# Taking 37 filler products out of the start of an attention and MoE kernel, and putting four ahead of it

## The chip, the cores and the metric

The kernel runs on one core of one Trainium2 chip. The metric is device time in microseconds (us), from one launch; smaller is better. Before the change the median of three runs is 240.69 us (239.54 to 241.6).

## The reference

What is computed is a Nyström approximation of attention over 8 batches of 8 heads (576 positions, head size 64, 32 landmarks), followed by a two-layer network with SiLU between its layers (512 to 2048 to 512). Cut to what matters:

```python
q_lm = q.reshape(B, H, m, S // m, D).mean(axis=3)      # m = 32 landmarks
k_lm = k.reshape(B, H, m, S // m, D).mean(axis=3)
A  = softmax(scale * q    @ k_lm.T)                    # 576 x 32 per head
Bm = softmax(scale * q_lm @ k_lm.T)                    # 32 x 32
C  = softmax(scale * q_lm @ k.T)                       # 32 x 576
Z  = Bm.T / (norm1(Bm) * norminf(Bm) + 1e-6)
for _ in range(6):
    Z = 2 * Z - Z @ Bm @ Z
x = A @ Z @ C @ v                                      # heads side by side: 4608 x 512
h = x @ w_in
out = (h * sigmoid(h)) @ w_out
```

All inputs and the output are float32; the kernel works in bfloat16 and float16 inside.

## The kernel before

The eight batches run one behind the other in a software pipeline. Of each batch, all 8 heads are kept as two groups of four heads by 32 landmarks, that is 128 partitions. In the first two batches TensorE forms the landmark sums itself; in later ones VectorE does, by adding halves.

**The order of the work is written out by hand.** The string `SEQUENCE` (lines 19 to 157) lists every step of every engine. `Plan.run` (line 204) walks through it, gives each step that needs PSUM the first free bank of seven (later eight), and hands the list to the program. Each engine executes its own steps in the order of the string and waits at each for its inputs; nothing is reordered. TensorE's weight load can run ahead of its products, its products can't run ahead of each other.

The names around the change, each with its batch behind the dot:

- `ldk` loads a block of keys (1) or queries (0) of batch 0 by SyncE's queue, in float32, into space that later holds `gm`; `kc` casts it, a part on ScalarE and a part on VectorE. `ld`, `ldv`, `wi` and `wo` load later batches, values and weights by GpSimd's queue.
- `lms` are the landmark sums: products of the identity with 64 columns of a position, summed in PSUM, six to a step. `tr` are transposes on TensorE (line 527), `trc` their copies to SBUF.
- `lmc` copies the sums, `ltr` transposes them by a product with the identity, `lmT` copies that. From `lmT` come the scores: `sb` (landmarks by landmarks), `A` (queries by landmarks) and `C` (landmarks by keys).
- `pb`, `Ax` and `Cx` are the exponentials on ScalarE (lines 647, 753, 798); `S` sums over a head on TensorE; `Ln` and `Rs` (lines 763, 767) turn the sums into reciprocals on ScalarE; `etn` is the normalized A.
- `ns`, `nsd` and `fb` are the six steps of the iteration for Z: a small product on TensorE, then two operations on VectorE, each waiting for the one before.
- `ctm` and `ctc` transpose and copy C's exponentials, `cv` is C by v, `wc` scales it, `zbd` and `zt` multiply it by Z, `m` multiplies that by `w_in`, and `mc` copies the result.
- `h` and `hx` are the first layer (A by `m`), `g` and `gx` its SiLU on ScalarE (lines 923 and 946). Behind them stands the second layer.

**Fillers.** A word such as `*5` in the string stands for five fillers, one behind the other (line 214). A filler is one product of a zero matrix (128 by 128) with 256 columns of zeros, written to PSUM bank 7, which no other step uses until the second layer begins. Nothing reads its result:

```python
    P.filler = Op("warm", [("PE", 0.11)],
                  lambda e: mm(banks[7][:, 0:256].rearrange("p (a x) -> p a x", a=2), zer,
                               bc(zer, 2, 1)))
```

Its operand `zer` is set once, by VectorE, at the start (line 445). A filler therefore waits for no other engine beyond that, and none waits for it; it only takes a place in TensorE's order. There are 64: 15 ahead of the first landmark sum `lms100.0`, six ahead of the sums of the second key block, six ahead of those of the first query block, and 37 behind `lms0112.0`, the last landmark sum of batch 0. In the profile a filler is a product on line 337 that writes `ps` and reads `zer`.

Of the kernel before, what the change touches and what calls it, by code (L numbers as in the profile page):

```python
# [28 lines left out]
ctc00.0/DVE tr05.1 trc05.1/ACT tr00.1 trc00.1/ACT Rs1.0 Rs0.0 ns11.0 nsd11.0 fb10.0 fb21.0 tr19.1
trc19.1/DVE ltr0.1 lms100.1 lms106.1 ns10.0 nsd10.0 lms1012.1 tr014.1 lms110.1 lms116.1  # L30
trc014.1/DVE ns21.0 tr114.1 lmT0.1/ACT wi1a wi0a wi1b1 wi1b0 wi3b0 wi3a lms1112.1 lmc1.1/ACT
tr10.1 trc10.1/ACT tr15.1 *2 ltr1.1 lmT1.1/ACT fb20.0 nsd21.0 etn1.0 trc15.1/DVE ns20.0 fb31.0 *3
ns31.0 ctm10.0 trc114.1/ACT etn0.0 nsd31.0 sb.1 pb.1 *1 A.1 Ax01.1 Ax00.1 nsd20.0 fb30.0 pbs.1
wrc.0 *1 ns30.0 nsd30.0 ctc10.0/DVE fb40.0 pbr.1 fb41.0 bmx.1 bmt.1 wi3b1 Ax11.1 Ax10.1 *5 C.1
Cx00.1 Cx11.1 Cx01.1 *1 ns40.0 nsd40.0 ns41.0 nsd41.0 fb50.0 fb51.0 cv0.0 cv1.0 wc.0 S01.1 Ln01.1
ns50.0 nsd50.0 *2 ns51.0 bbd.1 nsd51.0 zbd.0 S11.1 Ln11.1 S00.1 Ln00.1 wi2b0 wi2b1 wi2a ldv0.1
ldv1.1 *5 zt.0 ztc.0/DVE S10.1 ctm00.1 ctc00.1/DVE Rs0.1 Ln10.1 Cx10.1 *2 m1.0 mc11.0/ACT
mc10.0/DVE m0.0 f0.1 mc01.0/DVE mc00.0/ACT *1 ctm10.1 ctc10.1/DVE Rs1.1 csb.1 *1 h4.0 n1.1 m3.0
nrm.1 stz.1 stf0.1 mc31.0/DVE fb00.1 g4.0 mc30.0/DVE h2.0 g2.0 h6.0 g6.0 h0.0 g0.0 h3.0 ns00.1
wrc.1 nsd00.1 fb10.1 h5.0 g5.0 m2.0 mc21.0/ACT mc20.0/DVE *1 h13.0 g13.0 ns10.1 nsd10.1 fb20.1  # L40
h15.0 hx0.0 g15.0 ns20.1 nsd20.1 fb30.1 h9.0 g9.0 h11.0 g11.0 etn0.1 ns30.1 nsd30.1 fb40.1 hx8.0
gx8.0 g3.0 h8.0 h12.0 g12.0 etn1.1 ns40.1 nsd40.1 fb50.1 gx0.0 h10.0 g10.0 ld1.2 tr15.2
trc15.2/DVE h14.0 g14.0 ns50.1 nsd50.1 zbd.1 ldv2.1 cv0.1 wc.1 tr114.2 trc114.2/DVE tr19.2
trc19.2/DVE zt.1 g8.0 ztc.1/ACT tr10.2 trc10.2/DVE lra1.2 h7.0 g7.0 m3.1 mc31.1/ACT mc30.1/ACT
m1.1 mc11.1/DVE mc10.1/ACT h1.0 g1.0 ld0.2 tr00.2 lrb1.2 tr09.2 tr014.2 trc014.2/DVE tr05.2
trc05.2/DVE trc09.2/DVE lrc1.2 trc00.2/ACT h12.1 g12.1 h7.1 g7.1 h15.1 m2.1 mc20.1/ACT m0.1
mc00.1/ACT mc21.1/ACT mc01.1/ACT wo0 o0@5001.0 h14.1 g14.1 g15.1 o0@5000.0 fold lrd1.2 lra0.2
lrb0.2 lrc0.2 lrd0.2 h11.1 g11.1 ltr0.2 ltr1.2 lmT1.2/DVE lmT0.2/ACT ss00@5020.0 ss10@5020.0
ss20@5020.0 ss30@5020.0 wo1 h5.1 o1@5000.0 sb.2 pb.2 pbs.2 pbr.2 bmx.2 bmt.2 wo2 wt00 bbd.2 h8.1
h3.1 o1@5001.0 o2@5000.0 wo3 o2@5001.0 wt01 g8.1 csb.2 o3@5001.0 oc@5001.0/ACT g3.1 g5.1 n1.2  # L50
nrm.2 stz.2 o3@5000.0 hx8.1 f0.2 gx8.1 h0.1 g0.1 oc@5000.0/ACT h2.1 h10.1 g10.1 h4.1 h1.1 g2.1
g1.1 wt11 wt21 stf0.2 fb00.2 ns00.2 h13.1 g13.1 wt31 nsd00.2 fb10.2 wt10 wt20 wt30 p1@5020.0
c1@5020.0/ACT ns10.2 nsd10.2 fb20.2 h9.1 h6.1 g4.1 g9.1 g6.1 ss00@5100.0 p5@5020.0 c5@5020.0/DVE
hx0.1 gx0.1 ss10@5100.0 l1done.0 C.2 Cx00.2 Cx10.2 p6@5020.0 u2@5020.0/DVE ld100.3 ld101.3 ld110.3
ld111.3 ldv1.3 xt10.3<ldv1.3 xt11.3<ldv1.3 ns20.2 nsd20.2 ss20@5100.0 p3@5020.0 c12@5020.0
p7@5020.0 ld000.3 ld001.3 ld010.3 ld011.3 xt01.3<ldv1.3 xt00.3<ldv1.3 ldv0.2 ldv2.2 ldv1.2
l1done.1 A.2 Ax01.2 Cx11.2 ct1.2<ldv1.3 Ax10.2 Ax11.2 p1@5100.0 c1@5100.0/ACT Ax00.2 Cx01.2
ct0.2<ldv1.3 os@5000.0 ld100.4<ct0.2 ld101.4 ld110.4 ld111.4 lra1.3 fb30.2 ns30.2 p2@5020.0
# [1114 lines left out]
```

## Time and profile before

| | |
|---|---|
| runs | 240.69 us median, 239.54 to 241.6 |
| profiled execution, its own time | 239.41 us |
| its span, first to last instruction | 237.4 us |
| mean granted TensorE clock in the span | 0.996 |
| TensorE busy, fillers included | 231.4 us (97%) |
| ScalarE busy | 182.1 us (77%) |
| VectorE busy | 183.0 us (77%) |
| fillers, products | 64, median 273 ns each, from 1.1 to 31.0 us |

[...] "PE" is TensorE, "PEld" its weight loads, "DVE" VectorE, "ACT" ScalarE, "POOL" GpSimd, "SP" SyncE. Times in the views count from the start of the span. In the timeline a row merges equal instructions: start, length, engine, line, operation, what it writes and reads, and the count; in brackets how long the engine had been idle before it, and what ended that.

### The profile page before, as it was taken

The page shows a single profiled execution, that of the slowest core. Times are in us where ns is not written, and L with a number is a line of the kernel's source. Part 1 is how long each engine was busy: PE and PEld are TensorE (multiplying, and loading weights), DVE is VectorE, ACT ScalarE, POOL GpSimd, SP SyncE. Part 2 cuts the span into 40 slices and gives each one's busy share as a digit, 9 for nine tenths or more (in the row PEclk, how much of TensorE's full clock was granted, in tenths as well). Part 3 has the DMA queues.
Part 4 walks back from the last instruction along what each step waited for, and adds up shares of the span by engine and source line. Part 5 has one row for each costly group of instructions (what it writes and reads, how often), then busy time and mean ns, then how long its engine had stood idle before and what let it go on. Part 6 is the DMA issues. An engine that isn't in the chain of part 4 may idle for free.

```text
span 237.4 us, 7504 instructions
## 1 busy us (share of the span) xinstructions
PE 231.4 (97%) x2948; PEld 164.5 (69%) x2948; DVE 183.0 (77%) x508; ACT 182.1 (77%) x433; POOL 49.6 (21%) x89
## 2 busy tenths in 40 slices
PE   7999999999999999999999999999999999999993
PEld 5987556456877645687878655768876746789882
DVE  2689989898998669949999789858998665447752
ACT  3599999989889988996857998999779897812200
POOL 0936641240055004403060084000000000000000
PEclk9999999999999999999999999999999999999998
DMA  6999999999989996999999999995427450012355
GB/s 251 267 203 186 204 210 207 207 206 179 166 149 205 222 230 128 189 191 174 200 154 214 178 157 231 202 171 121 91 68 100 115 122 0 4 44 48 76 136 144
DMA packets 56163, 37.72 MB, mean 159 GB/s; under 512 B 37056, under 2 KB 47552, under 8 KB 56128
## 3 DMA queue, kind: packets, MB, share of 16 engines
q0 software_dynamic: 15168, 17.18, 44.4%
q1 hardware_dynamic: 40288, 19.28, 39.3%
q10 hardware_dynamic: 672, 0.79, 1.1%
q8 instruction: 23, 0.38, 0.7%
q14 instruction: 12, 0.10, 0.1%
HBM read 36.70 MB, written 9.44 MB: 194 GB/s over the span
## 4 chain that ended last, share of the span: by engine, by line
PE 84%; DMA 6%; ACT 4%; DVE 2%; SPq 2%; issue 1%; DVEq 0%; ACTq 0%
PE ps L337 81%; DMA out_dram<-ost 5%; PE ps L527 3%; SPq L988 2%; DMA gm<-in_k_dram 1%; DVE etn L772 1%; ACT L1126 1%; ACT ln L767 1%; ACT m L347 0%; ACT pb L652 0%; ACT ln L763 0%; ACT qk L347 0%; ACT et L753 0%; PE ps L813 0%; ACT gx L946 0%
## 5 line engine op out<-in xcount | busy, mean ns | idle before, releaser
L923 ACT ACTIVATE gm<-ps 128x512 f16<-128x512 f32 x128 | 68.1, 626 | 4.6 <-PE ps L337 4.4
L337 PE MATMUL ps<-etn,m 128*128 128x64 bf16 (+1 forms) x512 | 71.2, 286 | 0.1
L337 PEld LDWEIGHTS <-gm 128*128 128x128 f16 x512 | 48.8, 98 | 11.0 <-issue 1.0
L337 PE MATMUL ps<-w_out_sb,gm 128*128 128x256 f16 (+1 forms) x392 | 52.5, 281 | 0.0
L337 PEld LDWEIGHTS <-m 128*128 128x128 bf16 x512 | 31.4, 98 | 23.1 <-issue 2.8
L337 PEld LDWEIGHTS <-ss 128*128 128x128 f16 x408 | 38.4, 98 | 7.8 <-issue 1.8
L337 PE MATMUL ps<-wt,ss 128*128 128x256 f16 x272 | 34.9, 273 | 0.0
L1046 DVE TENSOR_TENSOR ost<-ost,ps 128x256 f32<-128x256 f32 x51 | 20.7, 416 | 10.5 <-PE ps L337 7.2
L347 ACT COPY ost<-ps 128x256 f32<-128x256 f32 (+1 forms) x45 | 17.3, 391 | 12.0 <-PE ps L337 11.8
L349 DVE CAST m<-ps 128x512 bf16<-128x512 f32 x29 | 18.8, 685 | 3.6 <-PE ps L337 3.5
L347 ACT CAST m<-ps 128x512 bf16<-128x512 f32 x35 | 18.9, 607 | 2.1 <-PE ps L337 2.1
L418 POOL DMA_DIRECT2D v<-in_v_dram x24 | 14.7, 621 | 27.9 <-PE ps L337 17.1
L721 DVE SCALAR_TENSOR_TENSOR st<-st,ps 128x128 bf16<-128x128 bf16 (+2 forms) x54 | 13.7, 257 | 7.8 <-PE ps L337 6.8
L401 POOL DMA_DIRECT2D qk<-in_k_dram x20 | 10.6, 545 | 36.6 <-DMA qT<-qk 16.5
L337 PE MATMUL ps<-w_out_sb,ss 128*128 128x256 f16 x136 | 17.6, 273 | 0.0
L349 DVE COPY ost<-ps 128x256 f32<-128x256 f32 x25 | 10.5, 421 | 7.1 <-PE ps L337 6.6
L946 ACT ACTIVATE gx<-ps 128x512 f16<-128x512 f32 x16 | 9.9, 622 | 7.5 <-PE ps L337 7.3
L337 PE MATMUL ps<-wt,gm 128*128 128x256 f16 x120 | 15.5, 272 | 0.0
L696 DVE TENSOR_TENSOR fb<-st,hmask 128x256 bf16<-128x256 bf16 (+1 forms) x54 | 14.5, 274 | 1.1
L401 POOL DMA_DIRECT2D qk<-in_q_dram x20 | 10.6, 548 | 20.3 <-issue 12.2
L798 ACT ACTIVATE ce<-ps 128x288 bf16<-128x288 f32 x32 | 12.9, 420 | 2.3 <-PE ps L337 2.3
L763 ACT ACTIVATE ln<-ps 128x288 f32<-128x288 f32 x32 | 12.3, 428 | 3.0 <-PE ps L337 2.8
(93 smaller groups left out, 347.6 us busy)
## 6 DMA issues: line engine op xcount, KB each, us to landing
out_dram<-ost SPq DMA_DIRECT2D x130, 64.0 KB, 2.0
v<-in_v_dram POOLq DMA_DIRECT2D x24, 192.0 KB, 7.7
qk<-in_k_dram POOLq DMA_DIRECT2D x20, 144.0 KB, 6.3
qk<-in_q_dram POOLq DMA_DIRECT2D x20, 144.0 KB, 6.1
w_out_sb<-in_moe_w_out_dram POOLq DMA_DIRECT2D x4, 512.0 KB, 15.1
gm<-in_k_dram SPq DMA_DIRECT2D x2, 576.0 KB, 3.9
gm<-in_q_dram SPq DMA_DIRECT2D x2, 576.0 KB, 6.8
qk<-in_q_dram POOLq DMA_DIRECT2D x2, 576.0 KB, 8.5
```

Source lines behind the costliest of these rows:

```text
L337: nc.tensor.matmul(out=out_ap, lhsT=lhsT, rhs=rhs, start=start, stop=stop, skip_group_check=True)
L347: nc.scalar.copy(out=out, in_=in_)
L349: nc.vector.tensor_copy(out=out, in_=in_)
L401: lambda e, t=t, g=g, h=h, src=src: nc.gpsimd.dma_start(out=qk_r[b % 2][64 * h:64 * h + 64, t, g].rearrange("p j d -> p (j d)"), in_=src[b ...
L418: lambda e, a=a: nc.gpsimd.dma_start(out=v_r[b % 2][a * L:(a + 1) * L, :, :], in_=v[b].rearrange("h (l a x) d -> a l h (x d)", l=L, a=VA)[ ...
L696: nc.vector.tensor_tensor(out=fb[it % 2][:, g0:g1], in0=bc(sr[it % 3][:, g0:g1, 0:L], 4, 2), in1=bc(hmask, n, 1), op=OP.mult), [o], 14.5 + ...
L721: nc.vector.scalar_tensor_tensor(out=s2[:, g0:g1, lo:SW], in0=s[:, g0:g1, lo:SW], scalar=2.0, in1=ps[:, 0:NG * SW].rearrange("p (g x) -> p ...
L763: lambda e, g=g, c=c, ln=ln: nc.scalar.activation(out=ln[:, c], in_=bank(me["S", g, c])[:, 0:HS], func=AF.Ln),
L798: nc.scalar.activation(out=ce[:, :, 0:VP].rearrange("p (i c) (a l) -> p c a i l", c=2, a=VA)[:, c], in_=bank(me["C"], 2 * g + c)[:, 0:HS]. ...
L923: lambda e, dc=dc, cell=cell: nc.scalar.activation(out=gm[:, dc, :], in_=bank(cell["o"]), func=AF.Silu),
L946: lambda e, d0=d0, cell=cell, c=c: nc.scalar.activation(out=gx[:, d0:d0 + 8, c:c + 64], in_=bank(cell["o"]).rearrange("p (c x) -> p c x", ...
L1046: nc.vector.tensor_tensor(out=out_, in0=x, in1=y, op=OP.add)
```

## The change

Only the string changes. All words with a star behind `lms0112.0` go: one filler ahead of `ltr0.0`, six ahead of `sb.0`, five ahead of `C.0`, two ahead of `ltr1.1`, three ahead of `ns31.0`, one each ahead of `A.1` and `ns30.0`, five ahead of `C.1`, one ahead of `ns40.0`, two ahead of `ns51.0`, five ahead of `zt.0`, two ahead of `m1.0`, one each ahead of `ctm10.1`, `h4.0` and `h13.0`. The first `*15` becomes `*19`. The two `*6` between them stay. So 31 fillers are left of 64. All other words keep their order, and so their PSUM banks; the rest of the diff is the text running over to other lines.

```diff
-ldk10 ldk11 ldk00 ldk01 const ident kc10ACT kc10DVE kj10 *15 lms100.0 tr15.0 tr10.0 trc10.0/DVE
+ldk10 ldk11 ldk00 ldk01 const ident kc10ACT kc10DVE kj10 *19 lms100.0 tr15.0 tr10.0 trc10.0/DVE
...
-lms0112.0 ld0.1<ldk11 ld1.1 ldv2.0 ldv0.0 wi0b1 ldv1.0 wi0b0 tr09.0 tr014.0 lmc0.0/DVE *1 ltr0.0
-lmT0.0/ACT *6 sb.0 pb.0 trc014.0/DVE trc09.0/DVE A.0 Ax01.0 Ax00.0 Ax10.0 Ax11.0 *5 C.0 Cx01.0
...
-tr10.1 trc10.1/ACT tr15.1 *2 ltr1.1 lmT1.1/ACT fb20.0 nsd21.0 etn1.0 trc15.1/DVE ns20.0 fb31.0 *3
-ns31.0 ctm10.0 trc114.1/ACT etn0.0 nsd31.0 sb.1 pb.1 *1 A.1 Ax01.1 Ax00.1 nsd20.0 fb30.0 pbs.1
-wrc.0 *1 ns30.0 nsd30.0 ctc10.0/DVE fb40.0 pbr.1 fb41.0 bmx.1 bmt.1 wi3b1 Ax11.1 Ax10.1 *5 C.1
-Cx00.1 Cx11.1 Cx01.1 *1 ns40.0 nsd40.0 ns41.0 nsd41.0 fb50.0 fb51.0 cv0.0 cv1.0 wc.0 S01.1 Ln01.1
-ns50.0 nsd50.0 *2 ns51.0 bbd.1 nsd51.0 zbd.0 S11.1 Ln11.1 S00.1 Ln00.1 wi2b0 wi2b1 wi2a ldv0.1
-ldv1.1 *5 zt.0 ztc.0/DVE S10.1 ctm00.1 ctc00.1/DVE Rs0.1 Ln10.1 Cx10.1 *2 m1.0 mc11.0/ACT
-mc10.0/DVE m0.0 f0.1 mc01.0/DVE mc00.0/ACT *1 ctm10.1 ctc10.1/DVE Rs1.1 csb.1 *1 h4.0 n1.1 m3.0
...
-wrc.1 nsd00.1 fb10.1 h5.0 g5.0 m2.0 mc21.0/ACT mc20.0/DVE *1 h13.0 g13.0 ns10.1 nsd10.1 fb20.1
...
+lms0112.0 ld0.1<ldk11 ld1.1 ldv2.0 ldv0.0 wi0b1 ldv1.0 wi0b0 tr09.0 tr014.0 lmc0.0/DVE ltr0.0
+lmT0.0/ACT sb.0 pb.0 trc014.0/DVE trc09.0/DVE A.0 Ax01.0 Ax00.0 Ax10.0 Ax11.0 C.0 Cx01.0 Cx10.0
...
```

More of the change, by code (lines that the diff above doesn't have):

```diff
@@ L23 @@
 lmT1.0/ACT trc00.0/DVE tr19.0 trc19.0/DVE trc15.0/DVE lms006.0 lms0012.0 lms010.0 lms016.0
-lms0112.0 ld0.1<ldk11 ld1.1 ldv2.0 ldv0.0 wi0b1 ldv1.0 wi0b0 tr09.0 tr014.0 lmc0.0/DVE *1 ltr0.0
-lmT0.0/ACT *6 sb.0 pb.0 trc014.0/DVE trc09.0/DVE A.0 Ax01.0 Ax00.0 Ax10.0 Ax11.0 *5 C.0 Cx01.0
-Cx10.0 Cx11.0 Cx00.0 pbs.0 pbr.0 bmx.0 bmt.0 csb.0 n1.0 nrm.0 tr09.1 lms000.1 lms006.1 S10.0
-lms0012.1 lms010.1 bbd.0 trc09.1/DVE stz.0 f0.0 stf0.0 stf1.0 fb00.0 lms016.1 Ln10.0 S00.0 Ln00.0
-fb01.0 lms0112.1 lmc0.1/DVE S01.0 ns00.0 nsd00.0 Ln01.0 S11.0 ns01.0 Ln11.0 nsd01.0 fb11.0 ctm00.0
+lms0112.0 ld0.1<ldk11 ld1.1 ldv2.0 ldv0.0 wi0b1 ldv1.0 wi0b0 tr09.0 tr014.0 lmc0.0/DVE ltr0.0
+lmT0.0/ACT sb.0 pb.0 trc014.0/DVE trc09.0/DVE A.0 Ax01.0 Ax00.0 Ax10.0 Ax11.0 C.0 Cx01.0 Cx10.0
+Cx11.0 Cx00.0 pbs.0 pbr.0 bmx.0 bmt.0 csb.0 n1.0 nrm.0 tr09.1 lms000.1 lms006.1 S10.0 lms0012.1
+lms010.1 bbd.0 trc09.1/DVE stz.0 f0.0 stf0.0 stf1.0 fb00.0 lms016.1 Ln10.0 S00.0 Ln00.0 fb01.0
+lms0112.1 lmc0.1/DVE S01.0 ns00.0 nsd00.0 Ln01.0 S11.0 ns01.0 Ln11.0 nsd01.0 fb11.0 ctm00.0
 ctc00.0/DVE tr05.1 trc05.1/ACT tr00.1 trc00.1/ACT Rs1.0 Rs0.0 ns11.0 nsd11.0 fb10.0 fb21.0 tr19.1
@@ L37 @@
-ldv1.1 *5 zt.0 ztc.0/DVE S10.1 ctm00.1 ctc00.1/DVE Rs0.1 Ln10.1 Cx10.1 *2 m1.0 mc11.0/ACT
-mc10.0/DVE m0.0 f0.1 mc01.0/DVE mc00.0/ACT *1 ctm10.1 ctc10.1/DVE Rs1.1 csb.1 *1 h4.0 n1.1 m3.0
-nrm.1 stz.1 stf0.1 mc31.0/DVE fb00.1 g4.0 mc30.0/DVE h2.0 g2.0 h6.0 g6.0 h0.0 g0.0 h3.0 ns00.1
-wrc.1 nsd00.1 fb10.1 h5.0 g5.0 m2.0 mc21.0/ACT mc20.0/DVE *1 h13.0 g13.0 ns10.1 nsd10.1 fb20.1
-h15.0 hx0.0 g15.0 ns20.1 nsd20.1 fb30.1 h9.0 g9.0 h11.0 g11.0 etn0.1 ns30.1 nsd30.1 fb40.1 hx8.0
-gx8.0 g3.0 h8.0 h12.0 g12.0 etn1.1 ns40.1 nsd40.1 fb50.1 gx0.0 h10.0 g10.0 ld1.2 tr15.2
@@ L43 @@
[L43 to L58, printed above, removed]
+tr10.1 trc10.1/ACT tr15.1 ltr1.1 lmT1.1/ACT fb20.0 nsd21.0 etn1.0 trc15.1/DVE ns20.0 fb31.0 ns31.0
+ctm10.0 trc114.1/ACT etn0.0 nsd31.0 sb.1 pb.1 A.1 Ax01.1 Ax00.1 nsd20.0 fb30.0 pbs.1 wrc.0 ns30.0
@@ new lines @@
+nsd30.0 ctc10.0/DVE fb40.0 pbr.1 fb41.0 bmx.1 bmt.1 wi3b1 Ax11.1 Ax10.1 C.1 Cx00.1 Cx11.1 Cx01.1
+ns40.0 nsd40.0 ns41.0 nsd41.0 fb50.0 fb51.0 cv0.0 cv1.0 wc.0 S01.1 Ln01.1 ns50.0 nsd50.0 ns51.0
+bbd.1 nsd51.0 zbd.0 S11.1 Ln11.1 S00.1 Ln00.1 wi2b0 wi2b1 wi2a ldv0.1 ldv1.1 zt.0 ztc.0/DVE S10.1
+ctm00.1 ctc00.1/DVE Rs0.1 Ln10.1 Cx10.1 m1.0 mc11.0/ACT mc10.0/DVE m0.0 f0.1 mc01.0/DVE mc00.0/ACT
+ctm10.1 ctc10.1/DVE Rs1.1 csb.1 h4.0 n1.1 m3.0 nrm.1 stz.1 stf0.1 mc31.0/DVE fb00.1 g4.0
+mc30.0/DVE h2.0 g2.0 h6.0 g6.0 h0.0 g0.0 h3.0 ns00.1 wrc.1 nsd00.1 fb10.1 h5.0 g5.0 m2.0
@@ new lines @@
+mc21.0/ACT mc20.0/DVE h13.0 g13.0 ns10.1 nsd10.1 fb20.1 h15.0 hx0.0 g15.0 ns20.1 nsd20.1 fb30.1
+h9.0 g9.0 h11.0 g11.0 etn0.1 ns30.1 nsd30.1 fb40.1 hx8.0 gx8.0 g3.0 h8.0 h12.0 g12.0 etn1.1 ns40.1
+nsd40.1 fb50.1 gx0.0 h10.0 g10.0 ld1.2 tr15.2 trc15.2/DVE h14.0 g14.0 ns50.1 nsd50.1 zbd.1 ldv2.1
+cv0.1 wc.1 tr114.2 trc114.2/DVE tr19.2 trc19.2/DVE zt.1 g8.0 ztc.1/ACT tr10.2 trc10.2/DVE lra1.2
+h7.0 g7.0 m3.1 mc31.1/ACT mc30.1/ACT m1.1 mc11.1/DVE mc10.1/ACT h1.0 g1.0 ld0.2 tr00.2 lrb1.2
+tr09.2 tr014.2 trc014.2/DVE tr05.2 trc05.2/DVE trc09.2/DVE lrc1.2 trc00.2/ACT h12.1 g12.1 h7.1
@@ new lines @@
+g7.1 h15.1 m2.1 mc20.1/ACT m0.1 mc00.1/ACT mc21.1/ACT mc01.1/ACT wo0 o0@5001.0 h14.1 g14.1 g15.1
+o0@5000.0 fold lrd1.2 lra0.2 lrb0.2 lrc0.2 lrd0.2 h11.1 g11.1 ltr0.2 ltr1.2 lmT1.2/DVE lmT0.2/ACT
+ss00@5020.0 ss10@5020.0 ss20@5020.0 ss30@5020.0 wo1 h5.1 o1@5000.0 sb.2 pb.2 pbs.2 pbr.2 bmx.2
+bmt.2 wo2 wt00 bbd.2 h8.1 h3.1 o1@5001.0 o2@5000.0 wo3 o2@5001.0 wt01 g8.1 csb.2 o3@5001.0
+oc@5001.0/ACT g3.1 g5.1 n1.2 nrm.2 stz.2 o3@5000.0 hx8.1 f0.2 gx8.1 h0.1 g0.1 oc@5000.0/ACT h2.1
+h10.1 g10.1 h4.1 h1.1 g2.1 g1.1 wt11 wt21 stf0.2 fb00.2 ns00.2 h13.1 g13.1 wt31 nsd00.2 fb10.2
@@ new lines @@
+wt10 wt20 wt30 p1@5020.0 c1@5020.0/ACT ns10.2 nsd10.2 fb20.2 h9.1 h6.1 g4.1 g9.1 g6.1 ss00@5100.0
+p5@5020.0 c5@5020.0/DVE hx0.1 gx0.1 ss10@5100.0 l1done.0 C.2 Cx00.2 Cx10.2 p6@5020.0 u2@5020.0/DVE
+ld100.3 ld101.3 ld110.3 ld111.3 ldv1.3 xt10.3<ldv1.3 xt11.3<ldv1.3 ns20.2 nsd20.2 ss20@5100.0
+p3@5020.0 c12@5020.0 p7@5020.0 ld000.3 ld001.3 ld010.3 ld011.3 xt01.3<ldv1.3 xt00.3<ldv1.3 ldv0.2
+ldv2.2 ldv1.2 l1done.1 A.2 Ax01.2 Cx11.2 ct1.2<ldv1.3 Ax10.2 Ax11.2 p1@5100.0 c1@5100.0/ACT Ax00.2
+Cx01.2 ct0.2<ldv1.3 os@5000.0 ld100.4<ct0.2 ld101.4 ld110.4 ld111.4 lra1.3 fb30.2 ns30.2 p2@5020.0
```

## The prediction

> **What bounds the kernel now.** I read the page's busy shares, slices and chain first, then TensorE in order of time over the first 34 us, then stretches of the span, then the fillers alone.
>
> ```profile
> span 237.4 us, 7504 instructions
> PE 231.4 (97%) x2948; PEld 164.5 (69%) x2948; DVE 183.0 (77%) x508; ACT 182.1 (77%) x433; POOL 49.6 (21%) x89
> ...
> PE   7999999999999999999999999999999999999993
> ...
> PEclk9999999999999999999999999999999999999998
> ...
> PE 84%; DMA 6%; ACT 4%; DVE 2%; SPq 2%; issue 1%; DVEq 0%; ACTq 0%
> ```
>
> TensorE looks busy from one end to the other, at full clock in every slice but the last, and 84% of the chain of waits lies on it. Fillers count as busy in that, so in the first 32 us, where all the fillers stand, this doesn't say that real work fills TensorE. Stretches of 3.4 us show what the other engines do there (columns: length, then busy time and instructions of TensorE, its weight loads, VectorE, ScalarE, GpSimd; clock; DMA). The length is my choice, between the 2.1 and 5.8 us that the clock took to change, derived below.
>
> ```profile
> 0.00:3.40 3.40, 2.34 (x12) 1.62 (x13) 0.91 (x9) 1.28 (x1) 0.49 (x5) 1.00 0.42 146
> 3.40:6.80 3.40, 2.79 (x30) 2.32 (x29) 0.70 (x2) 1.45 (x2) 0.77 (x1) 1.00 1.00 392
> 10.20:13.60 3.40, 3.39 (x76) 2.61 (x72) 2.60 (x9) 2.52 (x9) 2.01 (x3) 1.00 1.10 212
> 13.60:17.00 3.40, 3.40 (x82) 2.92 (x81) 2.97 (x16) 3.40 (x16) 1.04 (x2) 1.00 1.24 197
> 17.00:20.40 3.40, 3.40 (x76) 2.99 (x73) 3.23 (x13) 3.40 (x9) 2.63 (x5) 1.00 1.19 173
> 20.40:23.80 3.40, 3.40 (x109) 2.23 (x107) 3.23 (x18) 3.15 (x13) 1.77 (x4) 1.00 1.23 202
> 23.80:27.20 3.40, 3.40 (x50) 2.30 (x49) 2.94 (x11) 3.27 (x11) 1.44 (x3) 1.00 1.24 206
> 27.20:30.60 3.40, 3.33 (x25) 1.29 (x22) 3.30 (x12) 3.37 (x6) 3.38 (x5) 1.00 1.27 205
> ...
> 40.00:200.00 160.00, 159.73 (x1955) 108.81 (x1953) 132.25 (x356) 139.56 (x334) 29.63 (x54) 1.00 0.93 164
> ...
> 232.10:235.50 3.40, 1.28 (x12) 0.90 (x10) 0.85 (x2) 0.00 (x0) 0.00 (x0) 0.99 0.61 161
> ```
>
> From 13.6 to 20.4 ScalarE has no idle time (3.40 of 3.40 twice), and up to 30.6 little. It sets the pace there. From 40 to 200 TensorE is idle for 0.27 us of 160, so what is won or lost before 40 reaches the end. The same view of the fillers alone:
>
> ```profile
> 10.20:13.60 3.40, 1.67 (x12) 1.00 1.10 212
> 13.60:17.00 3.40, 0.09 (x1) 1.00 1.24 197
> 17.00:20.40 3.40, 0.73 (x5) 1.00 1.19 173
> 20.40:23.80 3.40, 1.56 (x10) 1.00 1.23 202
> 23.80:27.20 3.40, 1.84 (x11) 1.00 1.24 206
> 27.20:30.60 3.40, 0.17 (x1) 1.00 1.27 205
> ```
>
> Their busy time overlaps with that of their neighbours, and one that lies across a border counts in both rows. What a filler takes out of the stream of products comes from the timeline, as does the speed of a slow clock:
>
> ```profile
> 1.06 3.38 PE L337 MATMUL ps<-zer 128*128 128x256 bf16 x15 [1.06 <-DVE zer L445]
> 5.05 0.48 PE L337 MATMUL ps<-qk,idb 128*128 128x64 bf16 x6 [0.61 <-ACT qk L347]
> 5.34 1.15 PE L527 MATMUL ps<-idb,qk 128*128 128x128 bf16 x9
> ...
> 6.86 0.82 PE L337 MATMUL ps<-zer 128*128 128x256 bf16 x6
> ...
> 9.09 0.67 PE L527 MATMUL ps<-idb,qk 128*128 128x128 bf16 x9
> ...
> 232.35 1.04 PE L337 MATMUL ps<-wt,gx 128*128 128x256 f16 x8
> ```
>
> The first 15 fillers take 3.38 us and six at 6.86 take 0.82. With a last one of about 0.42 and 0.27, the spacing is (3.38 - 0.42)/14 = 0.21 us and (0.82 - 0.27)/5 = 0.11 us. Nine transposes take 1.15 us at 5.34 and 0.67 at 9.09. So the array ran at half speed until about 6.8, 5.8 us after its first product, though the clock column says 1.00 there.
>
> **The change part by part.** *The four fillers ahead.* At the slow spacing they take 4 x 0.21 = 0.84 us from 1.06 + 15 x 0.21 = 4.2 on, to 5.1, and the first landmark sum starts at 5.05: at most 0.06 us late. The work behind it waits for the last query block anyway, in the row at 9.60 below, where ScalarE sits idle 0.90 us for a transfer. I take 0; without that cover it would be 0.06. If a hole in TensorE's work holds the clock's rise back, closing it helps before 6.8 only, and the transfer at 9.60 hides that too.
>
> *The 37 fillers behind.* 37 x 0.11 = 4.1 us of TensorE's time. Most stood in a wait: the next real product had no data yet. Where one stood in the way shows here:
>
> ```profile
> 9.60 0.72 ACT L347 CAST qk<-gm 128x640 bf16<-128x640 f32 x1 [0.90 <-DMA gm<-in_q_dram]
> ...
> 11.10 0.42 DVE L349 CAST red<-ps 128x256 bf16<-128x256 f32 x1
> ...
> 11.57 0.27 PE L337 MATMUL ps<-zer 128*128 128x256 bf16 x1
> ...
> 11.68 0.28 PE L337 MATMUL ps<-idb,red 128*128 128x128 bf16 x2
> ...
> 11.79 0.82 PE L337 MATMUL ps<-zer 128*128 128x256 bf16 x6
> ...
> 11.99 0.37 ACT L347 CAST lmT<-ps 128x256 bf16<-128x256 f32 x1 [0.42 <-PE ps L337]
> ...
> 12.54 0.20 PE L337 MATMUL ps<-lmT 64*32 64x32 bf16 x4
> ...
> 12.97 1.32 ACT L753 ACTIVATE et<-ps 128x288 bf16<-128x288 f32 x4
> ...
> 14.15 0.44 ACT L798 ACTIVATE ce<-ps 128x288 bf16<-128x288 f32 x1
> ```
>
> At 11.57 a filler starts 0.05 us after VectorE's cast ends (11.52), and the products of that cast start 0.11 behind it: about 0.07 is saved, since a product elsewhere follows its release by 0.05 (cast of 4.27 to 5.00, product at 5.05). Of the next six, the last starts at 12.61 - 0.27 = 12.34 and streams until 12.45; the cast lmT ends at 12.36, and the score products could start at 12.41 in place of 12.54: 0.13. Together 0.2 us, on the path, since ScalarE idles 0.42 us ahead of that cast. The five at 12.97 save nothing: ScalarE's four exponentials fill 12.97 to 14.29, and the next kind starts at 14.15 from behind them. From there ScalarE is full, so the fillers that go up to 31 free a TensorE that waits for ScalarE. The sum of the plain effects is 0.2 us faster; its bounds are 0 (the 0.2 is lost in a later wait) and 4.1 (each filler on the path). I take 0.2, because ScalarE's busy rows say so.
>
> *What the fillers cover: the clock.* Without them TensorE has real holes. In 10.2 to 13.6 it loses 12 x 0.11 = 1.3 us, so it is busy (3.39 - 1.3)/3.4 = 61% instead of all the time; in 20.4 to 23.8 it is (3.40 - 1.1)/3.4 = 68%; in 23.8 to 27.2 it is (3.40 - 1.2)/3.4 = 65%; in 17.0 to 20.4 it is 84%. What does the clock do at 61 to 68%? The trace has one fall:
>
> ```profile
> 235.40:235.50 0.10, 0.00 (x0) 0.00 (x0) 0.00 (x0) 0.00 (x0) 0.00 (x0) 0.79 0.67 164
> ```
>
> A mean of 0.79 puts the fall from 1.00 to 0.50 at 235.46, that is 2.1 us after the last product (232.35 + 1.04 = 233.39); the 3.4 us that end there are 1.28/3.4 = 38% busy. At the start, 69% busy (2.34 of 3.40) didn't raise the clock and 82% (2.79) did. Each stretch that held full speed is 98% busy or more. So 61% lies between a row that fell (38%) and rows that held (98%), and is nearer to the first; 65 and 68% are about as near to either, and below the 69% that didn't raise it. I take it that the clock falls behind 13.6 and again behind 23.8. Bounds: never, or for a stretch behind each of the three.
>
> The price of a slow stretch of 3.4 us is the half of its work that isn't done, 1.7 us, less the idle time that it can use. Behind 13.6 the stretch is full (3.40 busy, one filler of 0.1): 1.7 - 0.1 = 1.6. Behind 23.8 the holes take 1.2, so 3.4 us cost 0.5; but this time TensorE also waits for ScalarE and VectorE, so the slow clock may last as long as the 5.8 us of the start, half of which, less 1.2, is 1.7. I take 1.3, nearer to the long end, because 69% busy didn't end the slow state of the start. **Sum: 1.6 + 1.3 - 0.2 = 2.7 us.** Against the profiled execution, whose time is 239.41 (2.0 around its span), that is 242.1; the median of the runs, 240.69, lies 1.28 above it, so I forecast 240.69 + 2.7 = 243.4. Alone, its range is 242.0 to 245.2: from a second stretch at 0.2 to a third slow stretch at 1.6, behind 27.2, where one filler goes.
>
> [...]
>
> **The rivals.** *No fall: not slower.* The holes are short, and the clock holds with 61 to 68%. For it: the longest hole is about 0.7 us (six fillers), a third of the 2.1 us before the one fall seen. Against it: those 2.1 us came with 38% of a stretch, and a mean over time doesn't ask for one long hole. Place: the stretches 10.2 to 13.6 and 20.4 to 27.2; it decides if the share at which the clock falls lies below 61%. Then only the 0.2 is left: 240.5. [...]
>
> *One fall.* Only one stretch drops, since where the stretches begin against the work needn't be the same each time: 1.6 or 1.3, less 0.2, so about 1.2 slower, 241.9. For it: 61% against 68%. Against: both lie on the same side of the start's 69%.
>
> *TensorE is the bound.* Each filler gives its time back, 4.1 us: 236.6. For it: the chain of waits, with 84% on TensorE. Against: ScalarE's full rows, and the cast lmT that ends at 12.36, behind the start of all six fillers.
>
> **How the numbers follow.** Forecast 0.52, no fall 0.26, one fall 0.17, TensorE the bound 0.05. One per cent is 2.4 us, about what a measurement of this kernel tells from no change (the runs shown spread over 239.54 to 241.6). The forecast lies just above this line; two thirds of its range do, so 0.35 of its 0.52 are slower and 0.17 the same; no fall gives 0.25 to the same and 0.01 to faster; one fall 0.12 to the same and 0.05 to slower; the last 0.05 are faster. Faster 0.06, same 0.54, slower 0.40. The range runs from 240.0, half a microsecond below the rival without a fall, to 245.2; it leaves out the fast rival, some scatter below 240.0, and the forecast's upper tail.
>
> **What would show it.** In the profile after: a clock column below 1.00 in stretches between 13 and 31, products there twice as far apart (nine transposes near 1.15 us and not 0.67), ScalarE waiting for TensorE between 13.6 and 20.4, where it now never does. The start of the score products at 12.3 in place of 12.54 shows the 0.2; the first landmark sum at 5.1 and the sums of the last query block still at 10.4 show that the four cost nothing. I'm wrong if the clock stays at 1.00 (then 240.5 holds), or if it falls and ScalarE's pace doesn't suffer, or if it stays low beyond 31, where each further 3.4 us would cost 1.7.

## The result, and the profile after

The change makes the kernel about 1% slower: 242.58 us median (241.66 to 243.95) against 240.62 (239.25 to 241.6) on the same chip, a ratio of 1.0101 with a 95% interval of 1.0075 to 1.0128 (nine executions of each). A second comparison, `after_again` below, gave 1.0077 (1.0041 to 1.0113). The forecast was 243.4, so time and sign came out. The reason did not: the early part, on which the prediction's sum rests, ends level with the kernel before, and the time is lost later. Now and then an execution of one of these kernels is disturbed and takes 244 to 250 us, and the ratios leave such executions out.

The page of the kernel after, its profiled execution (243.09 us):

```profile
span 241.2 us, 7438 instructions
PE 229.9 (95%) x2915; PEld 162.1 (67%) x2915; DVE 182.9 (76%) x508; ACT 182.3 (76%) x433; POOL 49.6 (21%) x89
...
PE   7898999999999989999989999999999999999990
...
PEclk9999799999999999999999999999999999999998
...
PE 80%; DMA 8%; DVE 5%; ACT 4%; issue 1%; SPq 1%; DVEq 0%
```

TensorE lost 33 products and is busy for 1.5 us less, but the span is 3.8 longer. Its row now shows an eight in slices 15 (84 to 90 us) and 21 (121 to 127), in a part of the kernel that the change doesn't touch, and DMA's share of the chain of waits went from 6 to 8%. The clock shows one dip, in slice 5. By stretches (length; busy time and instructions of TensorE, weight loads, VectorE, ScalarE, GpSimd; clock; DMA):

```profile
10.20:13.60 3.40, 2.88 (x74) 1.72 (x71) 2.78 (x10) 2.59 (x9) 2.13 (x4) 1.00 1.11 212
13.60:17.00 3.40, 3.37 (x71) 3.05 (x70) 3.01 (x15) 3.40 (x15) 0.42 (x1) 1.00 1.24 198
17.00:20.40 3.40, 3.01 (x70) 2.69 (x68) 3.23 (x13) 3.40 (x9) 2.69 (x6) 1.00 1.22 183
20.40:23.80 3.40, 3.17 (x101) 1.76 (x98) 3.30 (x20) 3.37 (x13) 1.62 (x3) 1.00 1.24 202
23.80:27.20 3.40, 2.78 (x33) 1.56 (x32) 2.42 (x9) 2.91 (x9) 2.75 (x5) 0.59 1.24 205
27.20:30.60 3.40, 3.40 (x28) 1.51 (x25) 3.30 (x11) 3.37 (x6) 2.69 (x4) 0.91 1.27 206
...
40.00:200.00 160.00, 157.87 (x1940) 107.39 (x1938) 131.52 (x355) 138.05 (x331) 29.55 (x54) 1.00 0.93 164
```

The clock fell once, behind 23.8 (0.59, then 0.91), and not behind 13.6. ScalarE is full from 13.6 to 20.4 as before. Between 40 and 200 TensorE is idle for 160 - 157.87 = 2.13 us, where it was 0.27. The timeline, at the places that matter:

```profile
1.06 3.63 PE L336 MATMUL ps<-zer 128*128 128x256 bf16 x19 [1.06 <-DVE zer L444]
...
5.18 0.34 PE L336 MATMUL ps<-qk,idb 128*128 128x64 bf16 x6 [0.49 <-ACT qk L346]
...
9.34 0.73 ACT L346 CAST qk<-gm 128x640 bf16<-128x640 f32 x1 [0.66 <-DMA gm<-in_q_dram]
...
11.79 0.37 ACT L346 CAST lmT<-ps 128x256 bf16<-128x256 f32 x1 [0.47 <-PE ps L336]
...
12.21 0.20 PE L336 MATMUL ps<-lmT 64*32 64x32 bf16 x4 [0.46 <-ACT lmT L346]
...
25.01 0.84 PE L812 MATMUL ps<-idb,ce 128*128 128x128 bf16 x6
...
87.06 0.56 PE L336 MATMUL ps<-v,ct 96*32 96x64 bf16 x48 [0.62 <-DMA ct<-ce]
...
122.03 0.36 PE L336 MATMUL ps<-v,ct 96*32 96x64 bf16 x24 [0.81 <-DMA ct<-ce]
122.68 0.36 PE L336 MATMUL ps<-v,ct 96*32 96x64 bf16 x24 [0.29 <-DMA ct<-ce]
```

The three waits at the end are new: the product C by v (`cv`) of batches 3 and 4 waits for `ct`, the DMA transpose of C's exponentials that SyncE issues from batch 2 on. No product of the kernel before waited for one. The following table is worked out from the records of both traces: start of a step, and how much later (+) it starts than in the kernel before.

```
step (engine)     before   after  after_again  f64_again   s33   e1_again  e4_out  e2_merged  e3_four
sb.0  (PE)         12.54   -0.32     -0.29       -0.28    -0.55    -0.21    -0.26    -0.18     -0.22
A.1   (PE)         21.28   -0.66     -0.61       -0.61    +0.02    +0.20    -0.35    -0.51     -0.11
m3.0  (PE)         27.75   +0.44     -0.55       +0.53    +0.63    +1.17    -0.24    -0.36     +0.52
ns10.1 (PE)        31.64   -0.01     -0.55       +0.08    +0.21    +0.75    -0.30    -0.42     +0.18
cv0.2 (PE)         69.20   +0.00     +0.41       +0.08    +0.21    +0.75    -0.09    -0.29     +0.19
cv0.3 (PE)         86.38   +0.68     +2.43       +0.08    +0.21    +0.74    +0.38    +1.66     +0.18
ns20.4 (PE)       120.66   +2.32     +2.89       +0.23    +0.21    +0.74    +0.63    +2.74     +0.18
cv0.7 (PE)        186.30   +2.32     +2.88       +0.22    +0.21    +0.74    +0.63    +2.75     +0.18
last product's end 233.38  +2.33     +2.89       +0.23    +0.21    +0.74    +0.63    +2.75     +0.18
from there to end    4.03   5.49      5.46        4.18     4.19     3.96     5.64     5.49      4.28
span              237.41  241.20    241.72      237.78   237.78   238.08   239.65   241.62    237.84
```

Read the column "after" down: 0.66 us is won up to 21, the slow clock takes it back by 31.6, nothing happens until 69, then 0.68 is lost at 87, 1.6 more by 121, and 1.46 behind the last product: 2.33 + 1.46 = 3.79, the growth of the span. These are sizes of one execution, and that of the kernel before lies 1.2 below its median, that of the kernel after 0.5 above its own, so the medians differ by 1.96 only. Of the 1.6 by 121, 0.3 comes at 116, in a wait for VectorE's `lmT`; the rest are the two waits at 122.

What lies at those places? Both traces show 23 DMA packets of 16,384 bytes on a queue marked "instruction" (q8, 0.38 MB in all). I take them for TensorE's own program: before, its 2948 products with as many weight loads make 5896 instructions, 256.3 to a packet. That a packet holds 256 is my estimate from this count and from the stops told below, which stand at one place in every 256 instructions. Without 33 products the program is 66 instructions shorter from batch 0 on, and each later load comes at another step. From the records of the traces, the start of the load and the loads' count from the first:

```
load         5       6       7       8       9      10      11      12      13      14      23
before    39.83   49.96   61.50   71.90   80.51   89.58  102.04  110.84  123.06  130.36  226.79
after     40.57   53.64   63.52   72.62   84.98   91.40  104.89  117.62  124.07  134.64  232.86
f64_again 40.14   49.85   61.60   72.19   80.71   89.08  102.75  110.75  121.54  132.20  226.82
s33       40.15   50.23   62.09   72.80   80.67   89.70  102.30  110.97  123.32  130.81  226.99
```

The transposes of batch 4 are issued at 114.5 and 115.8 before, with no load beside them, and at 116.4 and 117.8 after, with load 12 at 117.62. Time from issue to landing of `ct`, for the transposes issued between 113 and 121, before and after:

```profile
DMA to landing us min/median/max: 3.1/3.4/3.7
```

```profile
DMA to landing us min/median/max: 4.9/5.2/5.6
```

They take about 1.8 us longer. At 62 to 64 us the same happens with load 7: issue to landing of the two goes from 3.74 and 2.79 us to 4.86 and 3.91, and the longest 256-byte packet that starts between the second's issue and landing from 298 to 1361 ns.

For batch 3, whose wait at 87 us is the first loss, it isn't enough to ask whether a load lies beside a transpose: load 9 does so in both kernels. Before, it came at 80.51, ahead of the packets of both transposes, and the second landed 5.81 us behind its issue. After, it runs from 84.98 to 86.01, amid the packets: 467 packets of 256 bytes start from 85.0 to 85.5, then 5 and 17 in the next two half microseconds, some taking 1.4 us, and the second transpose lands after 7.22 us. GpSimd's transfers, the obvious other cause, had ended by 84.0. For batch 4 it is less clean: the packets that stall there, for up to 2.12 us, start at 118.90, 0.3 us behind the end of load 12, and GpSimd moved 269 KB beside the first transpose where it moved 126 before. How a load holds up the packets isn't shown.

The stores at the end are the second place. Issues of `out_dram` from 228 on, before and after:

```profile
L988 SPq DMA_DIRECT2D out_dram<-ost x12: 314/384/516, 228.2 to 234.8; - x12
L988 ACTq DMA_DIRECT2D out_dram<-ost x12: 322/432/512, 228.2 to 234.3; - x12
```

```profile
L987 SPq DMA_DIRECT2D out_dram<-ost x14: 314/420/1637, 228.3 to 238.4; - x14
L987 ACTq DMA_DIRECT2D out_dram<-ost x14: 322/430/1582, 228.3 to 238.0; - x14
```

One issue on each of the two queues takes 1.6 us where 0.52 was the longest (ns, shortest/median/longest), and load 23 now comes at 232.86, among these stores, where it came at 226.79.

### The profile page after: what moved, and what is told of

Its sections match the earlier page's. It is cut to its first block, busy times and chain, and to the rows that moved or that the text cites. A ratio compares the mean times of both kernels' runs of the same rounds, so it can differ in the third digit from the quotient of the medians.

```text
span 241.2 us, 7438 instructions
## 1 busy us (share of the span) xinstructions
PE 229.9 (95%) x2915; PEld 162.1 (67%) x2915; DVE 182.9 (76%) x508; ACT 182.3 (76%) x433; POOL 49.6 (21%) x89
## 4 chain that ended last, share of the span: by engine, by line
PE 80%; DMA 8%; DVE 5%; ACT 4%; issue 1%; SPq 1%; DVEq 0%
PE ps L336 77%; DMA ct<-ce 5%; DMA gm<-in_q_dram 3%; PE ps L526 2%; ACT gm L922 1%; DVE etn L771 1%; PE ps L812 1%; DVE st L720 1%; ACT L1125 1%; ACT gx L945 0%; DVE fb L695 0%; SPq L824 0%; ACT pb L651 0%; DVE wsb L855 0%; SPq L381 0%
## 5 line engine op out<-in xcount | busy, mean ns | idle before, releaser
L720 DVE SCALAR_TENSOR_TENSOR st<-st,ps 128x128 bf16<-128x128 bf16 (+2 forms) x54 | 13.6, 257 | 7.7 <-PE ps L336 6.8
```

Source lines behind the costliest of these rows:

```text
L720: nc.vector.scalar_tensor_tensor(out=s2[:, g0:g1, lo:SW], in0=s[:, g0:g1, lo:SW], scalar=2.0, in1=ps[:, 0:NG * SW].rearrange("p (g x) -> p ...
```

## The experiments

Two theories stood against the prediction's own (the clock): that TensorE's freed time or its holes move the later work, and that the **places of the instruction loads** decide. `e1`, `e2` and the four `s` kernels give a filler further widths:

```diff
+    P.filler = {w: Op("warm", [("PE", 0.11)], lambda e, n=n, a=a: mm(
+        banks[7][:, 0:a * n].rearrange("p (a x) -> p a x", a=a), zer, bc(zer[:, 0:n], a, 1)))
+                for w, n, a in (("*", 128, 2), ("~", 32, 1), ("=", 128, 4))}
```

so `~` is a product of 32 columns and `=` one of 512. Ratios are to the kernel before on the same chip.

**e3_four** and **e4_out**: the change's two parts, each alone.

```diff
-kc10ACT kc10DVE kj10 *15 lms100.0
+kc10ACT kc10DVE kj10 *19 lms100.0
```

> Only the four fillers ahead of the first landmark sum are added; all 37 others stay. Every theory: 240.6 us within 0.8, since the four lie beside the wait for the query block. The theory of the instruction loads allows a small shift either way, because TensorE's program is 8 instructions longer.

> Only the 37 later fillers are taken out; the first group stays at 15. Theory of the clock: as the change, 242.6 us, ratio 1.008. Theory of the instruction loads: near 242.6 as well (74 instructions fewer in place of 66, so the blocks lie 8 instructions from where the change has them); it allows a difference of some tenths. If the four were what costs, it would be 240.6 or less.

The four alone: 240.18 us, 1.0004 (0.9982 to 1.0026). The 37 alone (the change with `*15` kept): 241.44, 1.0062 (1.0032 to 1.0093). So the loss belongs to the 37, though `e4_out` lost less than the 242.6 expected. In the trace of `e4_out` the clock didn't fall ahead of the last product, and still 0.63 is lost up to the last product and 1.6 behind it (5.64 against 4.03).

**e1_small**: the 37 stay but stream 32 columns each. TensorE's time goes, the length of the program stays.

```diff
-tr09.0 tr014.0 lmc0.0/DVE *1 ltr0.0 lmT0.0/ACT *6 sb.0
+tr09.0 tr014.0 lmc0.0/DVE ~1 ltr0.0 lmT0.0/ACT ~6 sb.0
```

> The kernel before, but each of the 37 later fillers streams 32 columns of zeros in place of 256. TensorE's program keeps its length, so every 16 KB block of it is loaded at the same place in the program as before, while the holes in TensorE's work and the early gain are those of the change. Theory of the instruction loads (the loss comes from blocks of TensorE's program that are loaded at other places, beside the DMA transposes): about 240.6 us, ratio 1.000 within 0.004. Theory of the clock (the loss is the price of a slow stretch near 24): about 242.6, ratio 1.008. Theory of the early shift (the loads and transposes meet differently because the first 25 us run earlier): about 242.6 as well.

**e1_again**: the same kernel once more. Its profile is the one used here, as that of `f64_again` is further down.

> The kernel whose 37 later fillers are 32 columns wide, once more for a profile. Instruction loads: program as long as before, so behind 31 us no step moves against the kernel before by over 0.5 us; time 240.0 (239.2 to 241). Rival, TensorE's busy share ahead of 31 us decides: 242.5 as in the changed kernel.

239.83 us, 0.9997 (0.9975 to 1.0019), and 240.38, 1.0010 (0.9980 to 1.0039): no loss. Its column shows +0.75 by 31.6, from an effect told at the end, and then not 0.1 more: the expected half microsecond is missed, but it is missed early.

**e2_merged**: the opposite. The fillers are joined in pairs, 31 products in place of 64; the seven that stood alone behind the landmark sums go. The other holes stay filled, the program is 66 instructions shorter, as the changed one is.

```diff
-kc10ACT kc10DVE kj10 *15 lms100.0
+kc10ACT kc10DVE kj10 =7 *1 lms100.0
...
-Ax10.0 Ax11.0 *5 C.0
+Ax10.0 Ax11.0 =2 *1 C.0
```

> The kernel before, with the fillers merged in pairs into products of 512 columns and the seven single ones behind the landmark sums left out: 31 products in place of 64, so TensorE's program is as much shorter as by the change (33 products and 33 weight loads), but the holes stay filled and the clock stays up. Theory of the instruction loads: about 242.6 us, ratio 1.008. Theory of the clock: 240.6, ratio 1.000. Theory of the early shift: 240.6, since the first 25 us run as before.

243.3 us, 1.0117 (1.0075 to 1.0159). Its stretches:

```profile
10.20:13.60 3.40, 3.40 (x76) 2.04 (x80) 2.67 (x9) 2.59 (x9) 1.91 (x3) 1.00 1.10 211
...
23.80:27.20 3.40, 3.40 (x44) 1.84 (x42) 2.95 (x9) 3.32 (x10) 2.41 (x5) 1.00 1.24 206
...
40.00:200.00 160.00, 157.92 (x1933) 107.27 (x1931) 130.99 (x354) 137.46 (x330) 29.55 (x54) 0.99 0.95 164
```

TensorE is full and at full clock in both early stretches, the early steps are up to 0.5 us ahead, and behind 40 it is idle for 2.08 us, like the changed kernel; 1.88 of that is one wait of `cv` at 88.03, which ends 0.04 us behind the landing of batch 3's second transpose. The clock did fall later, from 89.79 to 93.21, right behind that wait, and in that stretch about 1.0 us more is lost. So the loss at the transposes and the one behind the last product (5.49 against 4.03) need neither holes nor a slow clock; only the step from +1.66 to +2.74 in the table goes with the clock.

**s16, s33, s65, s97**: the change, with 16, 33, 65 or 97 products of 32 columns spread over the places of the 37. Against the kernel before, the program is 34 instructions shorter, as long, 64 longer and 128 longer. One of the places, in `s33`:

```diff
-Ax10.0 Ax11.0 *5 C.0
+Ax10.0 Ax11.0 ~5 C.0
```

> As the change with 16 such small products put back: the program is 34 instructions shorter than before, half the change's shift. Theory of the instruction loads: somewhere from 0.998 to 1.012, decided by which transposes the blocks then meet; in the profile the loads of TensorE's blocks lie about half as far from their old places. Clock or early shift: 1.008 to 1.010, as the change.

> The changed kernel with 33 products of 32 columns put back into the places of the removed fillers, 19 fillers ahead as in the change: TensorE's program is exactly as long as before, the holes and the clock's risk are those of the change. Theory of the instruction loads: ratio 1.000 within 0.004 (about 240.2 us here). Clock or early shift: 1.008 to 1.010.

> As the change with 65 small products: the program is 64 instructions longer than before, about as far from it as the change, the other way. Theory of the instruction loads: a ratio that need not be 1.000 and need not be that of the change; a range from 0.995 to 1.015 over these four with at least 0.5% between its ends. Clock or early shift: 1.008 to 1.010; if small products cost time by themselves, a little over that of s33.

> As the change with 97 small products: 128 instructions longer than before, half a block of 256 away. Theory of the instruction loads: again a ratio of its own, within 0.995 to 1.015. Clock or early shift: 1.008 to 1.010; if small products cost time by themselves, over s65 by as much as s65 over s33.

| | instructions against before | us | ratio | start of ns10.1 | of cv0.7 | behind the last product |
|---|---|---|---|---|---|---|
| s16 | -34 | 241.40 | 1.0038 (1.0007 to 1.0068) | +1.31 | +1.30 | 5.03 |
| s33 | 0 | 239.68 | 0.9982 (0.9953 to 1.0012) | +0.21 | +0.21 | 4.19 |
| s65 | +64 | 242.23 | 1.0068 (1.0037 to 1.0098) | +1.45 | +1.52 | 4.20 |
| s97 | +128 | 245.29 | 1.0229 (1.0180 to 1.0277) | +3.51 | +5.79 | 4.29 |

With the length restored the loss is gone. The others tell more than "shorter is worse": in its trace `s65` loses next to nothing behind 31 us, so a shifted program isn't slow by itself; I take it that it depends on what the loads fall on. `s97` is longer than the kernel before and loses 2.3 us behind 31, 0.49 of it in a wait for a transpose at 126; its ratio lies above the 1.015 that was expected at most. But `s16`, `s65` and `s97` also lose 1.3 to 3.5 us ahead of 31. There TensorE stood still with its data ready:

```profile
22.30 0.30 PE L333 MATMUL ps<-qT,lmT 64*32 64x288 bf16 x2 [0.77 <-issue]
```

```profile
27.14 0.34 PE L809 MATMUL ps<-idb,ce 128*128 128x128 bf16 x3 [1.62 <-issue]
```

```profile
26.90 0.21 PE L333 MATMUL ps<-st,fb 128*128 128x32 bf16 x1 [2.37 <-issue]
```

These are s16, s65 and s97 in this order. "issue" means that nothing in the profile held it. Every such stop in all traces here, 13 of over 0.1 us, stands at the same place of the program, the 192nd instruction behind a multiple of 256, counted over products and weight loads; the one of `s65` is in the middle of six transposes that need nothing new. And a stop at the place n x 256 + 192 ends 1.3 to 1.6 us behind the landing of load n, in all 13 cases; where TensorE passed such a place without a stop, it was never sooner than 1.35 us behind load n (at least 1.40 in the kernel before, 1.56 in the kernel after). I take it that TensorE waited there for instructions: an estimate from these records, as no view names the wait.

The clock has a part in these times. In `s16` it was slow from 24.04 to 27.45, in `s97` from 26.53 to 29.95. The trace of `s65` has no such stretch, but it belongs to three executions of 240.3 to 241.1 us; the other seven, with a mean clock of 0.991 to 0.993, took 242.1 to 242.8.

**f64** and **f64_again**: the separation without small products in the holes. All 37 are out. The 31 left are cut into 64 shorter ones. All 64 stand ahead of the last landmark sum of batch 0, so it is from `h13.0` on (31 us), the place of the last of the 37, that each step has as many instructions ahead of it as in the kernel before. Between the two it has up to 74 more, and loads 1 to 4 come 1.5 to 4.5 us sooner.

```diff
-kc10ACT kc10DVE kj10 *15 lms100.0
+kc10ACT kc10DVE kj10 ~38 lms100.0
...
-lms106.0 lms1012.0 *6 kc11ACT
+lms106.0 lms1012.0 =13 kc11ACT
```

Here `~` has 128 columns and `=` has 118.

> All 37 later fillers are out and all holes stay open; the 31 fillers ahead are cut into 64 (38 of 128 columns in place of the 19, thirteen of 118 in place of each six), so that from the last landmark sum of batch 0 on TensorE's program has just as many instructions ahead of each step as in the kernel before. Theory of the instruction loads: behind 31 us every step keeps its distance from the kernel before to 0.3 us, the blocks from 39 us on are loaded within 0.5 us of where they were before, and the time is 240.4 (239.5 to 241.5), more only by what is lost ahead of 31 us. Rival, the missing fillers themselves move the work that follows: the distance grows by 2 us between 80 and 125 us as in the changed kernel, and the time is 242.5.

> The kernel with 64 short products ahead and all holes open, once more, since the profiled execution of its first run was disturbed. Instruction loads: behind 31 us no step moves against the kernel before by over 0.3 us, and the time is 239.9 (239.0 to 241.0), at most 0.3 us under the kernel before, by what the early steps win. Rival, missing fillers move the later work: 2 us more distance between 80 and 125 us.

239.91 us, 0.9978 (0.9953 to 1.0002), and 239.72, 0.9985 (0.9961 to 1.0009). Stretches of `f64_again`:

```profile
10.20:13.60 3.40, 2.86 (x78) 1.84 (x75) 2.75 (x10) 2.71 (x10) 1.93 (x3) 1.00 1.10 209
...
23.80:27.20 3.40, 2.78 (x33) 1.52 (x32) 2.42 (x9) 2.91 (x9) 2.38 (x5) 0.61 1.24 204
27.20:30.60 3.40, 3.40 (x27) 1.56 (x26) 3.30 (x12) 3.37 (x6) 2.94 (x5) 0.89 1.27 205
...
40.00:200.00 160.00, 159.74 (x1956) 108.75 (x1953) 132.29 (x357) 139.38 (x334) 29.56 (x54) 1.00 0.94 164
```

Ahead of 31 each step in the table stands within 0.1 us of the changed kernel: the same holes (2.86 against 2.88), the same fall of the clock (0.61 against 0.59). Behind it TensorE is idle for 0.26 us of 160, not for 2.13. The transposes of batch 4 are again issued at 116.4 and 117.8, but load 12 comes at 110.75, and their landing and the issues of the last stores are those of the kernel before:

```profile
DMA to landing us min/median/max: 2.8/3.0/3.2
```

```profile
L984 SPq DMA_DIRECT2D out_dram<-ost x12: 314/340/432, 228.4 to 235.1; - x12
L984 ACTq DMA_DIRECT2D out_dram<-ost x12: 322/414/455, 228.4 to 234.5; - x12
```

The rival that the missing fillers move the later work falls. Of the expectation's details one is missed: loads 11, 13, 14, 15 and 21 lie 0.7 to 1.8 us from where they were, not within 0.5; the column moves by no more than 0.15 us between 31.6 and the last product.

**after_again**: the changed kernel once more.

> The changed kernel once more. If its later loss belongs to the places of the blocks, which its program fixes, the loss comes at the same steps again: cv of batch 3 waits for its transpose near 87 us, cv of batch 4 near 122 us, in sum 2 us, time 242.5 (241.7 to 243.9). If it was chance, the places differ and the time lies anywhere from 240 to 244.

242.35 us. Stretch and timeline of its profiled execution (243.41 us):

```profile
23.80:27.20 3.40, 2.79 (x40) 1.42 (x37) 2.97 (x10) 3.34 (x10) 2.60 (x4) 1.00 1.24 206
```

```profile
24.88 0.50 PE L812 MATMUL ps<-idb,ce 128*128 128x128 bf16 x6
...
88.80 0.56 PE L336 MATMUL ps<-v,ct 96*32 96x64 bf16 x48 [1.96 <-DMA ct<-ce]
...
123.25 0.36 PE L336 MATMUL ps<-v,ct 96*32 96x64 bf16 x24 [0.28 <-DMA ct<-ce]
```

No fall of the clock this time, and the loss is larger: `cv` of batches 3 and 4 waits for its transposes again. It stands at +2.89 at the last product (a loss of 2 was expected) and takes 1.4 us more than before behind it. Another 1.0 was lost between 31.6 and 69, with waits of TensorE for the keys (0.42 us at 35.57) and the values (0.31 at 36.74) that GpSimd's queue brings. The place at the transposes repeats; the size moves between executions.

**What is shown.** Short program: loss at the transposes and the stores, with holes open (`after`, `after_again`, `e4_out`) or filled (`e2_merged`). Same length: none behind 31 us, with holes open (`f64_again`), filled with short products (`e1_again`, `s33`) or filled (`e3_four`, four products longer). Behind the last product it takes 5.46 to 5.64 us where load 23 starts 1.0 to 2.8 us ahead of that product's end, 5.03 where 3.6 us (`s16`), and 3.96 to 4.29 where 6.6 us or more. That the length of the program decides is shown by these runs. That a load slows the transpose or the store beside it is read from the records; no run moved a single load and nothing else. No version clearly beats the kernel before: all intervals of `f64` and `s33` contain 1.

## Why the prediction was right in time and wrong in cause

**"So what is won or lost before 40 reaches the end".** True where the program keeps its length (the columns of `f64_again`, `s33`, `e1_again` and `e3_four` are constant from 31.6 to the last product, to 0.15 us), false for the change: it is at -0.01 there and ends at +3.8. This step failed. TensorE's 0.27 us of idle time in 160 was read as robust; it was a schedule in which the transposes of batches 3 and 4 land only 1.4 to 2.0 us ahead of the products that read them, and the cost of the instruction loads beside them was no term of the sum, no rival, and in no range. That 243.4 lies near 242.58 is therefore mostly luck.

**The price of the slow clock, "1.6 + 1.3".** In the profile only the second fall came, and its price was mis-sized. `after` and `after_again` run the same program with and without it: at ns10.1 they stand at -0.01 and -0.55, so a slow stretch of 3.4 us cost 0.54 up to there (`f64_again`, from -0.61 to +0.08, agrees). By 69 even that is gone: `after_again` has lost its lead to late keys and values and stands at +0.41, `after` at 0.00. The products did run at half speed, as forecast: by the records the six transposes at 25.01 start 0.107 us apart, and 0.056 apart in the kernel before, whose row at the same step stands beside the 0.84 above:

```profile
21.66 1.32 ACT L753 ACTIVATE et<-ps 128x288 bf16<-128x288 f32 x4 [0.25 <-PE ps L337]
...
25.34 0.50 PE L813 MATMUL ps<-idb,ce 128*128 128x128 bf16 x6
```

but TensorE had holes and a lead of its own to pay with. Over whole executions the clock does count, beside the main loss. Of the sixteen of the kernel after, five with a mean clock of 0.982 to 0.990 took 243.26 us on average, and eleven with 0.995 or more took 242.26 (one of these, at 0.998, took 243.95). Of the 23 of the program of `f64`, five with 0.984 to 0.990 took 240.17 on average and the other eighteen 239.62. So slow stretches go with 0.5 to 1.0 us, but without them the kernel after is still over 1.5 us slower than the 240.62 before. Which way it works isn't shown: a wait for a transpose can come ahead of the fall, as in `e2_merged`.

**"Busy (3.39 - 1.3)/3.4 = 61%".** The stretch shows 2.88 of 3.40, 85%, and 20.4 to 23.8 shows 93% where 68 was worked out. Taking the spacing of a filler out of the busy time ignores that its neighbours' longer durations cover part of the hole (the transposes at 25.34 last 0.22 us each and start 0.056 apart). And a share doesn't settle it. In the 3.41 us that end at the fall, 20.99 to 24.40, TensorE was busy for 81%; it was busy for 69% from 24.52 to 27.94 in `e1_again` and for 55% from 25.61 to 29.03 in `s65`, and the clock held. These shares are worked out from the records; where the two stretches that held begin is my choice.

The trace of `after` places the clock's changes at 3.92, 24.40 and 27.81 us, 20.48 and 3.41 apart. The length of a single hole doesn't settle it either: in `after` TensorE's longest idle time around the fall is the 0.62 us that end at 24.60, and the clock fell; `s65` has a stop of 1.62 us, and the clock held. What makes the clock fall isn't shown by these runs.

**"Together 0.2 us".** The score products started at 12.21, forecast 12.3, and 0.05 us behind the cast (11.79 + 0.37 = 12.16) as worked out. Some of the 0.32 isn't the fillers': `e3_four`, which keeps all 37, starts them 0.22 early, its last query block having come earlier. Measured from the start of ScalarE's cast of that block, the gain is 0.07 us in `after` and 0.18 in `after_again` and `f64_again`, so 0.2 was about right. What was missed is the next gain: the row at 21.66 above has ScalarE wait 0.25 us for TensorE, which the prediction's "from there ScalarE is full" left out. In `after` that wait is gone and these exponentials start 0.64 earlier (21.02).

**The four fillers at 0.** Right: 1.0004 for `e3_four`. The first landmark sum starts at 5.18 and waits for ScalarE's cast, not for the fillers; behind it ScalarE still waits 0.66 us for the transfer at 9.34.

**The rivals.** "No fall" (240.5) has the clock right for `after_again` and the time wrong: that execution had no fall and took 243.41. "One fall" (241.9) is what the clock column of `after` shows, and is near its time by chance: its price up to 31.6 was 0.54, the lead cancelled it, and the loss came later. "TensorE is the bound" (236.6) had nothing for it: ScalarE is at 3.40 of 3.40 as before, and never waited for TensorE between 13.6 and 20.4, as the forecast's own test had asked.

**The range, "242.0 to 245.2".** Its ends don't follow from its terms: a second stretch at 0.2 gives 240.69 + 1.6 + 0.2 - 0.2 = 242.3, and a third at 1.6 gives 243.4 + 1.6 = 245.0. Nothing hung on the difference.

## What to carry to other kernels

Here, taking 33 products out at the start shifted, for the rest of TensorE's program, the steps beside which its blocks are loaded. So where a difference appears far behind the edit, compare the load times on the "instruction" queue of both traces before explaining it. To test whether removed work mattered itself, remove it once at constant instruction count (short dummies ahead of it) and once shorten the program with the work kept. An engine that is hardly idle (TensorE here, 0.27 us of 160) may still have transfers that land just in time (here 1.4 to 2.0 us ahead of their readers). And one profiled execution isn't the median: list the clocks of all executions beside their times.

## What the runs showed of the hardware that was not expected

- The packets of 16,384 bytes on the "instruction" queue, 256 instructions each by the estimate above, took 0.9 to 1.7 us in the traces of the kernels before and after. Of the 32 DMA transposes of a trace, those with a load between their issue and landing took 5.2 us on average to land and the others 3.4 (16 and 16, kernel after; 4.7 and 3.8, 15 and 17, before). Which transposes are hit isn't random, so this is no price of a load. With the loads at other steps, `after` went from -0.01 us at 31.6 to +2.33 at its last product.
- TensorE stopped with all its data ready, at the places told above, for 0.77 (`s16`), 1.62 (`s65`) and 2.37 us (`s97`), until 1.3 to 1.6 us behind the landing of a load; the kernels before and after, of nearly the same text, have no stop of over 0.1 us at such a place.
- The same program had a slow clock for 3.4 us in one execution (0.59 from 23.8 to 27.2 in `after`) and not in another (1.00 there in `after_again`).
